# Linear attention and two feed-forward blocks on one core: the first group's attention over 128 tokens at once

## The chip, the cores and the metric

The kernel runs on one core of one Trainium2 chip. The metric is the device time of one execution in microseconds (us); lower is better. Engines are named as the profile names them: PE multiplies matrices (PEld is its weight load), DVE, ACT and POOL work on vectors, SP issues most of the transfers.

## The reference

Three blocks follow each other, over 2 batches of 768 tokens: attention with decay over 8 heads of 64, a feed-forward block of 2048, and a second block with a product of two projections. All data are float32.

```python
for b in range(nb):                      # blocks of 64 tokens
    intra = np.einsum('bhic,bhjc->bhij', qb, kb) * Dmask[None]
    intra = np.einsum('bhij,bhjd->bhid', intra, vb)
    inter = np.einsum('bhid,bhde->bhie', qb * lam_pow[None], kv_state)
    out[:, :, sl] = intra + inter
    kb_dec = kb * rev_pow[None]
    kv_state = lam_block[None, :, None, None] * kv_state + np.einsum('bhsd,bhse->bhde', kb_dec, vb)
...
h = x @ w_in; x = np.maximum(0.01 * h, h) @ w_out
...
out = ((x @ w1) * (x @ w2) @ w3) @ w_out2
```

`Dmask[i, j]` is `lam ** (i - j)` at and below the diagonal, `lam_pow[i]` is `lam ** (i + 1)`, `rev_pow[i]` is `lam ** (63 - i)`, and `lam_block` is `lam ** 64`. Attention is the same function for any block length; a longer block has fewer state updates and a larger mask.

## The kernel before

The 1536 tokens are 12 chunks of 128 and 3 groups of 512 (4 chunks a group, `CPG`). The 8 heads are 4 pairs (`NPAIR`); the two heads of a pair (`j` = 0, 1) lie on the two halves of the partitions.

The whole program is a list of operations, each with its engines, a cost on each, a rank and the buffers that it takes. `in_order` (L64) plays them against those costs and writes each operation to an engine when the plan says that it can start; the engine's instructions then stand in that order, and each engine works strictly in it. `LATENCY["q"]` and `MB` are the planner's figures for a transfer. They set the order alone.

**Attention** is `attention(n, rank, joined)` for chunk `n`. The chunk's queries, keys and values come in two transfers of 512 KB (L365): queries and keys transposed (parts 0, 1), then keys and values (parts 2, 3). Each half of 64 tokens is worked by itself. `front` makes 16 score products and up to 16 state products `kd` x values (64x64 each, on PE). `mask` (L388) multiplies the scores by the decay table `dm` on DVE, `q_decay` (L394) and `k_decay` (L403) scale queries and keys. `fade` and `update` (L453, L461) bring the state from one half to the next. `outs` makes 16 products of masked scores with values and up to 16 of scaled queries with the state. From the second chunk of a group on, the front of chunk `n` is written between the output products of chunk `n-1` (`scores`, L433), two products of the one and two of the other in turn; the last chunk's outputs stand alone (`outputs`, L523). `done` splits the result into a rounded part (ACT, L505) and the rest (DVE, L161) in the group's `xy`, which the first feed-forward block reads.

**For the first group** the flag `early` keeps `k_decay` on ACT and `q_decay` and `fade` on DVE.

**The feed-forward blocks** run on products of 128x128 by 128x512, each three times (rounded x rounded, rest x rounded, rounded x rest). `unit_h` (`full`, L534) reads all of a group's `xy`; `unit_y` (`products`, L541) sums into four accumulators. The weights come as 512 KB each (L230); `convert` rebuilds float32 from raw bits in two ACT passes (L235) and three DVE passes (L239, L245, L254), and `weight` splits it again (ACT L157, then DVE or POOL L161). The 4 weights of a block of `w_in` and the 4 of `w_out` are used for the three groups in turn. Chunks 4 to 11 are worked between these products.

The table code runs before all this: `load_lam` (L169) on SP, `pool_consts` on POOL, and `table` (L202), a running product on DVE, for `dm` and `lpow`.

Of the kernel before, what the change touches and what calls it, by code (L numbers as in the profile page):

```python
# [14 lines left out]
P = 128  # L15
# [5 lines left out]
T = 512  # L21
# [22 lines left out]
class Op:  # L44
# [6 lines left out]
    def __init__(self, cost, fn, rank, after=(), takes=(), uses=(), behind=(), port=False):  # L51
        self.cost, self.fn, self.rank, self.takes, self.behind, self.port = cost, fn, rank, takes, behind, port
        self.after = [o for o in after if o is not None]
        self.end = self.ready = None
        for b in (*takes, *uses):
            b.users.append(self)
# [3 lines left out]
LATENCY = {"q": 2000}  # L60
MB = 2800


def in_order(ops, depth, fixed):  # L64
# [33 lines left out]
    while n:  # L98
        for e in left:
            while free[e] <= now:  # L100
                shut = free["port"] > now
                shared = lambda c: e == "pool" or e == "dve" and c.port
                o = next((c for c in left[e][:400] if not (shut and shared(c)) and can(c)), None)
                if o is None:
                    break
                free[e] = o.end = now + o.cost[e]
                if shared(o):
                    free["port"] = o.end
                o.seen = o.end + LATENCY.get(e, 60)
# [13 lines left out]
def tile_kernel(ctx: ExitStack, tc, qkv, lamb, w_in, w_out, w1, w2, w3t, wo, out):  # L123
# [43 lines left out]
    def load_lam(e):  # L167
        T_["lam"] = const.tile([P, NPAIR], F32, name="lam_sb")
        nc.sync.dma_start(out=T_["lam"], in_=lamb)  # L169

    def pool_consts(e):

        T_["ident"] = const.tile([P, 2, D], F32, name="ident")
        T_["zero"] = const.tile([P, D], F32, name="zero")
# [7 lines left out]
            out=T_["ident"][:, 0, :], in0=T_["ident"][:, 0, :], in1=T_["ident"][:, 1, :], op=ALU.add  # L182
# [14 lines left out]
    def table(name, tag, first, data):  # L197

        def fn(e):
            T_[name] = const.tile([P, 512], F32, tag=tag, name=name)[:, : NPAIR * D].rearrange("q (p i) -> q p i", i=D)  # L200
            for p in range(NPAIR):
                nc.vector.tensor_tensor_scan(  # L202
                    T_[name][:, p, :], T_["lam"][:, p : p + 1].to_broadcast([P, D]), data(), first, ALU.mult, ALU.add
                )
        return fn
# [147 lines left out]

    def attention(n, rank, joined):
# [38 lines left out]
        def q_decay(e):  # L393
            engines[e].tensor_tensor(  # L394
                out=new(qd, [P, NPAIR, 2, D]), in0=t(0),
                in1=T_["lpow"].unsqueeze(2).to_broadcast([P, NPAIR, 2, D]), op=ALU.mult,
            )

        def k_decay(e):
# [12 lines left out]
        early = n < CPG  # L412
        k_op = op(
            {"act": 1250} if early else {"dve": 640, "pool": 1250, "act": 1250}, k_decay, rank,
            [ld[1], tables[0]], [kd], [inp], port=True,
        )
        q_op = op(
            {"dve": 640} if early else {"dve": 640, "pool": 1250}, q_decay, rank + 1, [ld[0], tables[1]], [qd], [inp],
            port=True,
# [46 lines left out]
        for c in range(2 if carry else 1):  # L466
# [3 lines left out]
            if old:  # L470
                fo = op({"dve": 420} if early else {"act": 1000, "dve": 420, "pool": 700}, fade(k, c), rank + 0.4, [st_op[k], tables[1]], port=True)
# [5 lines left out]
        px = Buf("acc" if early else "ps")  # L477
# [21 lines left out]
        def done(xo, behind=()):  # L499
            part = lambda v: xs[g].tile[:, v, :, c0 * CH : (c0 + 1) * CH]  # L500
            src = lambda: px.tile.rearrange("q p c i -> q p (c i)")
            r = xo.rank + 0.8

            def x_hi(e):
                nc.scalar.copy(part(0), src())  # L505

            o1 = op({"act": 580}, x_hi, r, [xo], [], [px, xs[g]])
            o2 = op({"dve": 660}, lo(lambda: part(1), lambda: part(0), src), r, [o1], [], [px, xs[g]], behind)
            x_ops[g] += [o1, o2]
            x_done[n] = xo  # L510
# [202 lines left out]
    def unit_o(g, f, rank):  # L713
# [32 lines left out]

    consts = op({"dve": 100}, dve_consts, 0)
    lam_op = op({"q": 400}, load_lam, 0.5)
    pc = op({"pool": 600}, pool_consts, 0)
    tables = [  # L750
        op({"dve": 900}, table("dm", "w34_6", 0.0, lambda: T_["ident"][:, 0, :]), 0, [lam_op, pc]),
        op({"dve": 900}, table("lpow", "w34_7", 1.0, lambda: T_["zero"]), 1, [lam_op, pc]),
    ]
    PLACE = {0: "yf0", 1: "yf1", 2: "yf2", 5: "yf1", 6: "yf2", 8: "yf1", 9: "yf2"}
    for n in range(CPG):
        attention(n, 10 * n, n > 0)
    outputs(CPG - 1, 10 * CPG)
# [4 lines left out]
    CHUNKS = {0: {4: 1, 5: 6}, 1: {6: 1, 7: 6}, 2: {8: 1}, 3: {9: 11}, 4: {10: 6}, 5: {11: 1}}  # L762
    for k in range(2):
# [34 lines left out]
def _lay_out(q, k, v, lam, moe_w_in, moe_w_out, moe2_w1, moe2_w2, moe2_w3, moe2_w_out):  # L798
# [15 lines left out]
    lamb = np.empty((P, NPAIR), lam.dtype)  # L814
    lamb[:D] = lam[0::2]
    lamb[D:] = lam[1::2]
# [29 lines left out]
```

## Time and profile before

| | |
|---|---|
| median of 3 runs | 559.92 us (558.36 to 560.97) |
| span of the profiled execution, first to last instruction | 556.9 us |
| that execution's own time | not recorded apart from the span; the three timed runs are 1.5 to 4.1 us longer than it |
| PE busy | 539.2 us, 97% of the span, 3680 products |
| DVE, ACT, POOL busy | 316.3, 301.4, 65.5 us |
| transfers | 54.07 MB, 97 GB/s in the mean |

Times in the rows below are us from the span's start. A row of the timeline gives start, length, engine, line, what is written and read, how many instructions it merges, and in brackets the idle time before it with what ended it. "issue" there means that the engine waited for nothing that the profile shows. Two engines' rows overlap freely; a busy engine that others wait for is what to look for.

### The profile page before, as it was taken

What the parts mean: (1) busy time and instruction counts of PE and PEld (TensorE: products, weight loads), DVE (VectorE), ACT (ScalarE), POOL (GpSimd) and SP (SyncE); (2) the same over time, 40 slices, a digit from 0 to 9 for tenths busy, and PEclk for the clock granted to TensorE, in tenths of its full rate; (3) what the DMA queues carried; (4) which work ended last, traced back from release to release, by engine and by line L of the source; (5) the groups of instructions that cost most, each with busy time, mean ns of one, the idle gap of its engine ahead of it and who ended that gap; (6) DMA issues with size and microseconds to landing.
All of it is one profiled execution on the core that took longest, in us unless ns stands there. A gap on an engine that the chain in (4) does not pass through costs nothing.

```text
span 556.9 us, 9041 instructions
## 1 busy us (share of the span) xinstructions
PE 539.2 (97%) x3680; PEld 447.1 (80%) x3680; DVE 316.3 (57%) x524; ACT 301.4 (54%) x540; POOL 65.5 (12%) x58
## 2 busy tenths in 40 slices
PE   5599999999999999999999999999999999999997
PEld 4488878888888888888888888888888888888885
DVE  4887798870348951699716778883233333343331
ACT  4787798892238742586724667763335333343331
POOL 0121040000000000020101201110003111120110
PEclk9899999999999999999999999999999999999999
DMA  8983845450004430146501324420002000020002
GB/s 287 385 286 107 288 171 191 150 185 5 0 4 142 157 114 0 39 151 207 171 1 38 114 79 149 151 77 0 1 0 77 1 1 0 2 75 1 0 0 77
DMA packets 15882, 54.07 MB, mean 97 GB/s; under 512 B 1888, under 2 KB 2144, under 8 KB 15840
## 3 DMA queue, kind: packets, MB, share of 16 engines
q1 hardware_dynamic: 15696, 53.36, 27.8%
q8 instruction: 29, 0.48, 0.3%
q10 hardware_dynamic: 144, 0.13, 0.1%
q14 instruction: 13, 0.11, 0.1%
HBM read 50.33 MB, written 3.15 MB: 96 GB/s over the span
## 4 chain that ended last, share of the span: by engine, by line
PE 89%; DMA 4%; DVE 3%; ACT 2%; issue 1%; SPq 1%; ACTq 0%
PE ps L534 45%; PE acc L541 34%; PE ps L672 8%; DMA raw<-in_w_in_dram 2%; DMA raw<-in_w_out_dram 1%; DMA yf<-in_qkv_dram 1%; PE ps L433 1%; PE ps L523 1%; DVE u L245 1%; ACT faded L449 1%; PE acc L433 1%; SPq L365 1%; DVE wa L161 0%; DVE f L254 0%; DVE rp L239 0%
## 5 line engine op out<-in xcount | busy, mean ns | idle before, releaser
L534 PE MATMUL ps<-xy,wp 128*128 128x512 f32 x756 | 179.1, 390 | 0.1
L534 PEld LDWEIGHTS ps<-xy,wp 128*128 128x128 f32 x756 | 141.8, 188 | 30.1 <-DVE a L388 0.5
L541 PE MATMUL acc<-act,wa 128*128 128x512 f32 x396 | 96.0, 390 | 0.0
L534 PE MATMUL ps<-xy,wa 128*128 128x512 f32 x396 | 95.5, 391 | 0.3 <-ACT wa L157 0.3
L534 PEld LDWEIGHTS ps<-xy,wa 128*128 128x128 f32 x396 | 74.0, 188 | 16.5 <-ACT wa L157 0.7
L541 PEld LDWEIGHTS acc<-act,wa 128*128 128x128 f32 x396 | 74.1, 188 | 15.5
L161 DVE TENSOR_TENSOR act<-ps,act 128x512 fp32r<-128x512 f32 x72 | 49.4, 686 | 59.0 <-ACT act L549 58.9
L541 PE MATMUL acc<-wp,act 128*128 128x512 f32 x276 | 66.6, 389 | 0.0
L157 ACT CAST wp<-wa 128x512 fp32r<-128x512 f32 x48 | 29.8, 622 | 63.8 <-PE ps L534 39.2
L235 ACT ACTIVATE rp<-raw,bp 128x512 f32<-128x512 uint16 x72 | 54.7, 764 | 15.2 <-DVE f L254 15.0
L541 PEld LDWEIGHTS acc<-wp,act 128*128 128x128 f32 x276 | 51.8, 188 | 10.7
L235 ACT ACTIVATE rn<-raw,bn 128x512 f32<-128x512 uint16 x72 | 54.6, 761 | 10.6 <-DMA raw<-in_w3t_dram 4.5
L570 ACT ACTIVATE ps<-ps 128x512 f32<-128x512 f32 x48 | 27.9, 580 | 57.8 <-PE ps L534 57.7
L239 DVE SCALAR_TENSOR_TENSOR rp<-rp,rn 128x512 uint32<-128x512 f32 x72 | 53.2, 740 | 4.5 <-ACT rp L235 3.8
L161 DVE TENSOR_TENSOR wp<-wa,wp 128x512 fp32r<-128x512 f32 x36 | 24.9, 691 | 49.7 <-ACT wp L157 49.7
L549 ACT CAST act<-ps 128x512 fp32r<-128x512 f32 x72 | 42.0, 583 | 5.6 <-DVE ps L708 2.9
L541 PE MATMUL acc<-act,wp 128*128 128x512 f32 x180 | 43.5, 391 | 0.0
L541 PEld LDWEIGHTS acc<-act,wp 128*128 128x128 f32 x180 | 33.6, 188 | 7.0
L254 DVE SCALAR_TENSOR_TENSOR f<-rp,u 128x512 uint32<-128x512 uint32 x56 | 38.6, 695 | 0.5
L245 DVE TENSOR_SCALAR u<-raw 128x512 uint32<-128x512 uint32 x72 | 34.0, 473 | 3.0 <-DMA raw<-in_w_in_dram 2.5
L708 DVE TENSOR_TENSOR ps<-ps,ta 128x512 f32<-128x512 f32 x24 | 16.8, 699 | 28.7 <-PE ps L534 28.7
L161 DVE TENSOR_TENSOR wp<-f,wp 128x512 fp32r<-128x512 f32 x24 | 16.6, 690 | 26.6 <-ACT wp L157 26.6
(92 smaller groups left out, 524.5 us busy)
## 6 DMA issues: line engine op xcount, KB each, us to landing
raw<-in_w_in_dram SPq DMA_DIRECT2D x16, 512.0 KB, 4.4
raw<-in_w_out_dram SPq DMA_DIRECT2D x16, 512.0 KB, 4.1
raw<-in_w3t_dram SPq DMA_DIRECT2D x16, 512.0 KB, 4.2
raw<-in_w_dram SPq DMA_DIRECT2D x16, 512.0 KB, 3.3
yf<-in_qkv_dram SPq DMA_DIRECT2D x14, 512.0 KB, 6.1
inp<-in_qkv_dram SPq DMA_DIRECT2D x10, 512.0 KB, 6.7
raw<-in_wo_dram SPq DMA_DIRECT2D x8, 512.0 KB, 4.1
out_dram<-f SPq DMA_DIRECT2D x11, 256.0 KB, 2.0
```

What stands on the lines that cost most here:

```text
L157: return lambda e: nc.scalar.copy(dst(), src())
L161: engines[e].tensor_tensor(out=dst(), in0=src(), in1=hi_().bitcast(F32), op=ALU.subtract)
L235: nc.scalar.activation(out=new(buf, [P, 512]), in_=top, func=AF.Relu, scale=8.0, bias=T_[bias])
L239: nc.vector.scalar_tensor_tensor(out=rp.tile.bitcast(U32), in0=rp.tile, scalar=32768.0, in1=rn.tile, op0=ALU.min, op1=ALU.add)
L245: nc.vector.tensor_scalar(out=new(u, [P, 512], U32), in0=mid, scalar1=2.0**-13, scalar2=2.0**19 - 1, op0=ALU.mult, op1=ALU.min)
L254: nc.vector.scalar_tensor_tensor(out=get().bitcast(U32), in0=rp.tile.bitcast(U32), scalar=16, in1=u.tile, op0=ALU.logical_shift_left, op1= ...
L534: nc.tensor.matmul(o, w(a)[:, cc * P : (cc + 1) * P], x(b, cc), start=k == 0, stop=k == 3 * NCC - 1)
L541: nc.tensor.matmul(o, st(a), mv(b), start=first and k == 0, stop=last and k == 2)
L549: nc.scalar.copy(buf.tile[:, 0, :], ps.tile)
L570: nc.scalar.activation(out=ps.tile, in_=ps.tile, func=AF.Prelu, alpha=0.01)
L672: nc.tensor.matmul(ps.tile, w(a)[:, k * P : (k + 1) * P], wo_part[j](b), start=j == 0 and n == 0, stop=j == NF2 - 1 and n == 2,)
L708: lambda e: nc.vector.tensor_tensor(out=pb.tile, in0=pb.tile, in1=ta.tile, op=ALU.mult),
```

## The change

Chunks 0 to 3 get a function of their own, `first_attention`, with all 128 tokens of a chunk as one block. Scores are 8 products of 128x128 for a chunk, the state 8 of 64x64 (over 128 tokens), the outputs 8 of 64x128 from the masked scores and 8 of 64x128 from the state. There is one fade and one state update for a chunk. Masks are two DVE operations of 512 a partition, with two new tables `wide0` and `wide1` of 128 columns a pair; `lpow` gets 128 columns too, and `dm` is built later. `k_decay` takes 8 ACT operations of 64 instead of 4 of 128. `q_decay` and `fade` may go to POOL. No front is written between another chunk's outputs any more. `lamb` is loaded from ACT's queue, with 12 columns instead of 4. The host lays out parts 2 and 3 of the first four chunks with 128 tokens on the partitions. The weight `("in", 0)` gets rank 25, and the planner's two transfer figures change.

```diff
-LATENCY = {"q": 2000}
-MB = 2800
+LATENCY = {"q": 3600}
+MB = 2900
...
-        nc.sync.dma_start(out=T_["lam"], in_=lamb)
+        nc.scalar.dma_start(out=T_["lam"], in_=lamb)
...
+    def wide_table(j):
+        def fn(e):
+            T_["wide", j] = const.tile([P, NPAIR, CH], F32, name=f"wide{j}")
+            for p in range(NPAIR):
+                k = NPAIR + 2 * p + j
+                nc.vector.tensor_tensor_scan(
+                    T_["wide", j][:, p, :], T_["lam"][:, k : k + 1].to_broadcast([P, CH]),
+                    T_["ident"].rearrange("q x y -> q (x y)"), 0.0, ALU.mult, ALU.add,
+                )
...
+    def first_attention(n, rank):
...
+        def scores(e):
+            for j in range(2):
+                new(sc[j], [P, NPAIR, CH])
+            for p in range(NPAIR):
+                for j in range(2):
+                    h = half[j]
+                    mm(sc[j].tile[:, p, :], rows(1)[h, p, :], rows(0)[h, p, :], start=True)
+        fr = op({"pe": 1300}, scores, rank, [ld[0]], [*sc], [inp])
...
+        masked = [op({"dve": 660}, mask(j), rank, [fr, wide[j]], [a[j]], [sc[j]]) for j in range(2)]
...
+            q_op = op({"dve": 640, "pool": 1250}, q_decay, rank + 1, [ld[0], tables[1]], [qd], [inp], port=True)
...
+        k_op = op({"act": 2100, "dve": 800}, k_decay, rank + 1, [ld[1], *wide], [kd], [inp], port=True)
...
+                for j in range(2):
+                    mm(st.tile[half[j], 0, p, :], kd.tile[:, p, j, :], heads(3)[:, p, j, :], start=True)
+        st_mm = op({"pe": 700}, sums, rank + 1, [k_op], [st], [inp, kd])
...
+            fo = op({"act": 1000, "dve": 420, "pool": 700}, fade, rank + 0.4, [st_op[2 * n], tables[1]], port=True)
...
+        st_op[2 * n + 2] = op({"dve": 420}, update, rank + 0.5, [st_mm, fo, x_done.get(n - 2)], [], [st])
...
+            for kind in ("v", "state") if inter else ("v",):
+                for p in range(NPAIR):
+                    for j in range(2):
+                        o = px.tile[half[1 - j], p, :]
+                        if kind == "v":
+                            mm(o, heads(3)[:, p, j, :], a[j].tile[:, p, :], start=p == 0)
+                        else:
+                            mm(o, state(2 * n)[half[j], p, :], qd.tile[half[j], p, :], start=False)
...
     for n in range(CPG):
-        attention(n, 10 * n, n > 0)
-    outputs(CPG - 1, 10 * CPG)
+        first_attention(n, 10 * n)
...
+    weight("in", 0, 0, 25)
```

Where the order moves, in the places that the prediction speaks of:

PE, from the last chunk of the first group to the second wide product block, before (`acc<-a` and `acc<-qd` are chunk 3's outputs, `ps<-inp` and `ps<-inp,kd` chunk 4's front, `ps<-xy,wa` is `unit_h`):

```order
L523 MATMUL acc<-a,inp 64x64 x2
L523 MATMUL acc<-qd,state_115 64x64 x2
L433 MATMUL ps<-inp 64x64 x16
L433 MATMUL ps<-inp,kd 64x64 x16
L534 MATMUL ps<-xy,wa 128x512 x24
```

The same place now (L393 is the first group's attention: `acc<-a` and `acc<-ta` are chunk 3's outputs from its two masks; its eight state products, `acc<-inp,kd`, stand two rows above this piece):

```order
L393 MATMUL acc<-ta,inp 64x128
L393 MATMUL acc<-a,inp 64x128
L393 MATMUL acc<-ta,inp 64x128
L393 MATMUL acc<-a,inp 64x128
L393 MATMUL acc<-ta,inp 64x128
L393 MATMUL acc<-a,inp 64x128
L393 MATMUL acc<-ta,inp 64x128
L393 MATMUL acc<-qd,state_117 64x128 x8
L676 MATMUL ps<-xy,wa 128x512 x12
L585 MATMUL ps<-inp 64x64 x16
L585 MATMUL ps<-inp,kd 64x64 x16
L676 MATMUL ps<-xy,wa 128x512 x12
```

Chunk 4's front now follows the first `unit_h` instead of preceding it, and 120 small products stand ahead of that block (8+8+8 for the first chunk and 8 more for each other), where 248 of chunks 0 to 3 and 32 of chunk 4 stood.

ACT, from chunk 3's `k_decay` to the last rounding of the first group's `xy`, before:

```order
L403 ACTIVATE kd_349<-inp_258,dm_125 128x2x64 x4
L505 CAST xy_199<-acc_279 128x4x128
L157 CAST wa_362<-f_355 128x512
L235 ACTIVATE rp_366<-raw_273,bp_101 128x512
L235 ACTIVATE rn_370<-raw_273,bn_103 128x512
L235 ACTIVATE rp_443<-raw_345,bp_101 128x512
L235 ACTIVATE rn_446<-raw_345,bn_103 128x512
L403 ACTIVATE kd_451<-inp_357,dm_125 128x2x64 x4
L505 CAST xy_199<-acc_378 128x4x128
L403 ACTIVATE kd_468<-yf1_373,dm_125 128x2x64 x4
L235 ACTIVATE rp_512<-raw_460,bp_101 128x512
L235 ACTIVATE rn_515<-raw_460,bn_103 128x512
```

and now:

```order
L427 ACTIVATE kd_305<-inp_217,wide0_126 128x64 x4
L427 ACTIVATE kd_305<-inp_217,wide1_132 128x64 x4
L453 ACTIVATE faded1_122<-state1_117,lpow_149 128x64 x4
L158 CAST wa_364<-f_343 128x512
L502 CAST xy_208<-acc_324 128x4x128
L251 ACTIVATE rp_387<-raw_253,bp_103 128x512
L251 ACTIVATE rn_391<-raw_253,bn_105 128x512
L502 CAST xy_208<-acc_369 128x4x128
```

Before, the `k_decay` of chunks 4 and 5 and five more weight passes stood ahead of the last rounding; now a fade, one weight split and two weight passes do.

## Rows read from the trace of the kernel before

**Rows 1.** The page: busy times, PE in 40 slices, the queue of instructions.

```profile
PE 539.2 (97%) x3680; PEld 447.1 (80%) x3680; DVE 316.3 (57%) x524; ACT 301.4 (54%) x540; POOL 65.5 (12%) x58
...
PE   5599999999999999999999999999999999999997
...
q8 instruction: 29, 0.48, 0.3%
```

**Rows 2.** Waits of PE from 0 to 31 us: total, times, longest.

```profile
PE ps L433 <- DMA yf<-in_qkv_dram: 5.3, 2, 4.9
PE acc L433 <- issue: 4.4, 2, 3.6
PE ps L433 <- ACT kd L403: 1.3, 1, 1.3
PE acc L523 <- issue: 1.2, 1, 1.2
```

**Rows 3.** Timeline of PE, single rows between 4 and 42 us.

```profile
4.94 1.97 PE L433 MATMUL ps<-yf 64*64 64x64 f32 x32 [4.94 <-DMA yf<-in_qkv_dram]
...
22.57 0.37 PE L433 MATMUL acc<-qd,state 64*64 64x64 f32 x2 [3.61 <-issue]
...
28.62 0.98 PE L433 MATMUL ps<-inp 64*64 64x64 f32 x27
29.43 1.10 PE L433 MATMUL ps<-inp,kd 64*64 64x64 f32 x32
30.46 5.75 PE L534 MATMUL ps<-xy,wa 128*128 128x512 f32 x24
...
41.49 3.01 PE L534 MATMUL ps<-xy,wa 128*128 128x512 f32 x12 [0.31 <-ACT wa L157]
```

**Rows 4.** Windows: length, busy (instructions) of PE, PEld, DVE, ACT, POOL, clock, DMA share, GB/s.

```profile
0.00:16.38 16.38, 8.12 (x222) 7.55 (x222) 8.60 (x24) 7.24 (x17) 1.10 (x8) 1.00 0.85 305
16.38:22.56 6.18, 2.35 (x127) 2.08 (x127) 4.91 (x11) 4.85 (x10) 0.00 (x0) 0.99 1.02 402
22.56:28.03 5.47, 4.24 (x127) 4.11 (x128) 4.25 (x9) 4.10 (x11) 1.71 (x2) 0.70 0.92 348
```

**Rows 5.** Windows after the wide products began, same columns.

```profile
30.46:100.00 69.54, 69.17 (x1130) 56.75 (x1127) 57.96 (x102) 56.49 (x121) 11.89 (x10) 1.00 0.60 207
100.00:310.00 210.00, 210.00 (x928) 173.96 (x927) 126.30 (x208) 115.70 (x194) 12.14 (x9) 1.00 0.27 88
```

**Rows 6.** Timeline of ACT, 17 to 35 us.

```profile
17.58 1.28 ACT L403 ACTIVATE kd<-inp,dm 128x128 f32<-128x128 f32 x4 [1.59 <-DMA inp<-in_qkv_dram]
18.77 0.56 ACT L505 CAST xy<-acc 128x512 fp32r<-128x512 f32 x1
19.23 0.62 ACT L157 CAST wa<-f 128x512 fp32r<-128x512 f32 x1
19.75 0.76 ACT L235 ACTIVATE rp<-raw,bp 128x512 f32<-128x512 uint16 x1
20.41 0.75 ACT L235 ACTIVATE rn<-raw,bn 128x512 f32<-128x512 uint16 x1
...
33.62 1.05 ACT L449 ACTIVATE faded<-state,lpow 128x64 f32<-128x64 f32 x4
34.58 0.57 ACT L570 ACTIVATE ps<-ps 128x512 f32<-128x512 f32 x1
```

**Rows 7.** Timeline of DVE and POOL, single rows.

```profile
5.17 0.84 DVE L202 TENSOR_TENSOR_SCAN dm<-lam_sb,ident 128x64 f32<-128x64 f32 x4 [4.21 <-DMA lam_sb<-in_lamb_dram]
...
29.49 0.69 DVE L161 TENSOR_TENSOR xy<-acc,xy 128x512 fp32r<-128x512 f32 x1 [0.34 <-ACT xy L505]
...
71.48 1.76 POOL L394 TENSOR_TENSOR qd<-inp,lpow 128x512 f32<-128x512 f32 x1 [12.37 <-issue]
```

**Rows 8.** The chain that ended last: wide blocks of 12, start, length.

```profile
87.30 2.95 PE acc L541 x12
...
100.65 2.72 PE acc L541 x12
```

More of the change, by code (lines that the diff above doesn't have):

```diff
@@ L44, with __init__ @@
 class Op:
-    def __init__(self, cost, fn, rank, after=(), takes=(), uses=(), behind=(), port=False):
+    def __init__(self, cost, fn, rank, after=(), takes=(), uses=(), behind=(), port=False, lag=None):
         self.cost, self.fn, self.rank, self.takes, self.behind, self.port = cost, fn, rank, takes, behind, port
@@ L108, in in_order @@
                     free["port"] = o.end
-                o.seen = o.end + LATENCY.get(e, 60)
+                o.seen = o.end + (o.lag or LATENCY.get(e, 60))
                 n -= 1
@@ L181, in pool_consts @@
         nc.gpsimd.tensor_tensor(
-            out=T_["ident"][:, 0, :], in0=T_["ident"][:, 0, :], in1=T_["ident"][:, 1, :], op=ALU.add
+            out=T_["ident64"], in0=T_["ident"][:, 0, :], in1=T_["ident"][:, 1, :], op=ALU.add
         )
@@ L195, in dve_consts, with table @@
         nc.scalar.activation(out=T_["warm"], in_=T_["bp"], func=AF.Relu)
-    def table(name, tag, first, data):
+    def table(name, tag, first, data, wide):
         def fn(e):
-            T_[name] = const.tile([P, 512], F32, tag=tag, name=name)[:, : NPAIR * D].rearrange("q (p i) -> q p i", i=D)
+            T_[name] = const.tile([P, 512], F32, tag=tag, name=name)[:, : NPAIR * wide].rearrange(
+                "q (p i) -> q p i", i=wide
+            )
             for p in range(NPAIR):
                 nc.vector.tensor_tensor_scan(
-                    T_[name][:, p, :], T_["lam"][:, p : p + 1].to_broadcast([P, D]), data(), first, ALU.mult, ALU.add
+                    T_[name][:, p, :], T_["lam"][:, p : p + 1].to_broadcast([P, wide]), data(), first, ALU.mult, ALU.add
+                )
+        return fn
+    def wide_table(j):
[6 more added lines that the diff above has]
+                    T_["ident"].rearrange("q x y -> q (x y)"), 0.0, ALU.mult, ALU.add,
                 )
@@ L354, in attention, with x_split, x_hi @@
+    def x_split(n, xo, px, src, behind=()):
+        g, c0 = divmod(n, CPG)
+        part = lambda v: xs[g].tile[:, v, :, c0 * CH : (c0 + 1) * CH]
+        r = xo.rank + 0.8
+        def x_hi(e):
+            nc.scalar.copy(part(0), src())
+        o1 = op({"act": 580}, x_hi, r, [xo], [], [px, xs[g]])
+        o2 = op({"dve": 660}, lo(lambda: part(1), lambda: part(0), src), r, [o1], [], [px, xs[g]], behind)
+        x_ops[g] += [o1, o2]
+        x_done[n] = xo
     def attention(n, rank, joined):
@@ L395, in q_decay @@
                 out=new(qd, [P, NPAIR, 2, D]), in0=t(0),
[L396 removed]
+                in1=T_["lpow"][:, :, :D].unsqueeze(2).to_broadcast([P, NPAIR, 2, D]), op=ALU.mult,
             )
@@ L470, in attention @@
             if old:
-                fo = op({"dve": 420} if early else {"act": 1000, "dve": 420, "pool": 700}, fade(k, c), rank + 0.4, [st_op[k], tables[1]], port=True)
+                fo = op({"act": 1000, "dve": 420, "pool": 700}, fade(k, c), rank + 0.4, [st_op[k], tables[1]], port=True)
             st_op[k + 1] = op({"dve": 420}, update(k + 1, c, old), rank + 0.5, [fr, fo, x_done.get(n - 2)], [], [st])
@@ L499, in done @@
         def done(xo, behind=()):
[L500 to L510, printed above, removed]
+            x_split(n, xo, px, lambda: px.tile.rearrange("q p c i -> q p (c i)"), behind)
         pend[n] = {
@@ L813, in _lay_out @@
     qkv = np.stack([transposed(q), transposed(k), natural(k), natural(v)], axis=2)
-    lamb = np.empty((P, NPAIR), lam.dtype)
-    lamb[:D] = lam[0::2]
-    lamb[D:] = lam[1::2]
+    for part, a in ((2, k), (3, v)):
+        whole = a.reshape(B, NPAIR, 2, NCHB, CH, D).transpose(0, 3, 4, 1, 2, 5).reshape(nch, P, 512)
+        qkv[:CPG, :, part] = whole[:CPG]
+    lamb = np.empty((P, NPAIR + H), lam.dtype)
+    lamb[:D, :NPAIR] = lam[0::2]
+    lamb[D:, :NPAIR] = lam[1::2]
+    lamb[:, NPAIR:] = lam
     w_in = moe_w_in.reshape(NPAIR, 2, D, F1)[:, ::-1].reshape(DM, F1)
```

99 lines of the change are left out of this document (88 added, 11 removed).

## The prediction

> **What bounds the kernel now.** Read the page first. PE is busy for 97% of the span, and its slices are full from the third on; only the first two, 28 us, have room [rows 1]. Then the windows: from 30.46 us, where the first wide product starts [rows 3], to 100 us PE is busy 69.17 of 69.54 us, and from 100 to 310 us all of the time [rows 5]. So the time is the moment at which the wide products start plus PE's own work behind it, 556.9 - 30.46 = 526.4 us with the last copies. The change can gain ahead of 30.46 us, and lose by giving PE more work or a wait behind it.
>
> Ahead of it the list of waits names what PE lacks [rows 2]: 5.3 us for queries, keys and values (4.9 of them the first load), 1.3 us for scaled keys, and 5.6 us (4.4 + 1.2) of "issue", in which neither data nor a semaphore is late. The windows show where these pauses sit: cut at their ends, they hold 222+222 = 444, then 127+127 = 254, then 127+128 = 255 instructions of PE and PEld [rows 4]. The page has 7360 of them over the kernel and 29 packets of 0.48 MB in the queue of instructions, 254 instructions and 16.5 KB for each [rows 1]. So PE stops where a new packet of its code is due, and does so while it runs through small products quickly and the transfers run at 402 GB/s. [...]
>
> **The new chain to the first wide product.** Loads keep their order and their bytes, and they run at the limit of the transfers (402 GB/s [rows 4]: 524 KB in 1.30 us), so I leave them where they are; without `lam`, SP is free 0.4 us sooner at most, which I count as nothing. Chunk 3's last half lands at 17.58 us: there ACT's wait ends and `kd` begins [rows 6]. From then on ACT's own list, in the order shown above, leads to the end:
> - `kd`, 8 operations of 64, and a fade, 4 more. Four such operations take 34.58 - 33.62 = 0.96 us to the next instruction [rows 6]: 3 x 0.96 = 2.88 us, to 20.46.
> - a weight split, 19.75 - 19.23 = 0.52 us, and the rounding of chunk 2's outputs, 19.23 - 18.77 = 0.46 us: to 21.44.
> - two weight passes of 20.41 - 19.75 = 0.66 us: to 22.76.
> - the rounding of chunk 3's outputs, 0.56 us, to 23.32, and on DVE the rest, 0.69 us [rows 7]: 24.0.
>
> PE must have chunk 3's outputs ready by 22.76. The trace has no 128-column form of these products. The nearest row is a front at the full clock, 32 instructions in 1.10 us [rows 3], which are 8 pairs of 64 columns, 0.14 us a pair; with twice the columns I take 0.28. The low end is 0.14 (length costs nothing), the high end about 0.5 (the two heads do not overlap, or all runs as slowly as the first 32, 1.97 us [rows 3]: 0.25 a pair, doubled 0.49). At 0.28, chunk 3's state products take 4 x 0.14 = 0.55 us from 19.50 (`kd` ready), its outputs 8 x 0.28 = 2.2 us: 22.3, within 0.5 us of late.
>
> On that stretch lies one more packet of code. 120 small products make 480 instructions ahead of the first wide one, where 280 made 1120, so of three pauses one is left, near the 445th instruction. That is in chunk 3's outputs. It can cost 0 (the packet is there) to 3.61 us. I take 0.5 us behind what ACT's list covers: the pause at the same count was the short one, 4.4 - 3.6 = 0.8 us [rows 2], and about 0.5 is covered, but the products now come to it faster. The wide products then start at 24.5 us, 5.96 us earlier.
>
> [...]
>
> **What is covered.** Tables: four running products of 64 columns take 0.84 us [rows 7]; the two wide tables and `lpow` have twice the columns, 0.84 to 1.68 us each, so all are done by 5.2 + 3 x 1.68 = 10.2 us at the latest, and the loads of the last two chunks hide it; the end hangs on chunk 3, at 16.3 us and later. `q_decay` on POOL takes up to 1.76 us [rows 7] where DVE took less; chunk 3's queries land one transfer before 17.58, at 16.3, and are wanted near 21.2. If POOL's two fades come first, 1 us of that cover goes and nothing shows. DVE's list up to the last rest (two masks, an update, two rests, three weight passes, none over 0.7 us) runs beside ACT's 5.7 us.
>
> **What moves behind the start.** Chunk 4's front, 30.46 - 28.62 = 1.84 us [rows 3], stood ahead of the wide products and now stands among them: all of it is added. It also makes two more changes between small and wide products: a block of 12 beside such a change takes 2.95 us, one without 2.72 [rows 8], so 0.23 us. The other chunks keep their products.
>
> **The sum.** -5.96 + 1.84 + 0.23 = -3.9 us: 556.9 becomes 553.0. The timed runs lie 1.5 to 4.1 us above the span, 3.0 for the median, which I carry over: 559.9 - 3.9 = **556.0 us**. No change, for a measurement of this kernel, is within 0.5%, 2.8 us.
>
> **The rivals.**
>
> *The small products stay slow, and the kernel is slower.* At the lower clock, or with the two heads of a pair one after the other, a 128-column pair takes the high end, 0.49 us. Scores, outputs and state outputs are then 1.97 us each for a chunk, the state products 0.98. Four chunks take 25.6 us, less a state output for the first; the second chunk lands six transfers of 1.30 us before 17.58, at 9.8 us, and 23.6 us are left then. PE ends at 33.4, the wide products start at 34.6, 4.2 us late, and with the 2.07 us behind them the time is 566.2. It decides from the third chunk on: each chunk at that speed costs 3.4 us more, so two of them eat the gain. For it: the first 32 instructions took 1.97 us against 1.10 later [rows 3], though the granted clock reads 1.00 there [rows 4]. Against it: PE ran at speed in the window up to the long pause, 127 products in 2.35 us [rows 4], with waits for loads and weights before that it will have less of, and it slowed only behind 3.61 us of nothing. [...]
>
> *The pause of code stays at full length.* With 3.6 us at the 445th instruction, reached near 21 us, outputs end at 25.9 instead of 22.3, and the wide products start at 27.1: -3.4 + 2.07 = -1.3 us, 558.6. For it: the longest pause of before came at the same rate of transfers [rows 4].
>
> *The conversions become the bound.* The wide products start 6 us earlier, but the weights are still converted at ACT's pace. Per two weights ACT has four passes, two splits and two operations on the result, 4 x 0.66 + 2 x 0.52 + 2 x 0.57 = 4.8 us, and per chunk `kd`, a rounding and two fades, 1.19 + 0.46 + 1.92 = 3.6 us [rows 6]: 8.4 us against PE's 2 x 2.72 + 1.84 = 7.3. Four such steps lose 4.4 us, of which the two `kd` that the new order gives to POOL take 2.4 away: 2.0 to 4.4 us lost, 558.0 to 560.4. For it: the one wait of the wide products is for a weight, 0.31 us [rows 3], with DVE busy 57.96 and ACT 56.49 of 69.54 us [rows 5].
>
> **How the numbers follow.** The forecast gets 0.60, the slow products 0.11, the pause 0.13, the conversions 0.16. The forecast's own range: 0 for the code pause and 0.5 us less on ACT give 555.0, transfers 0.4 us sooner and first wide products that begin on the rounded part alone, 0.69 us before the rest [rows 7], give 553.9, and the scatter of the runs of before, about 1 us, 553; upward, pause and cover together 1.5 us, 557.5. To hold 8 in 10 the range reaches over the pause and the conversions and leaves most of the slow products out: 553.0 to 560.4. Faster by over 0.5% (below 557.1) is 0.54 of the forecast and 0.04 of the pause and the conversions, where they come in part: 0.58. Within 0.5% is the rest of these, 0.06 + 0.25 = 0.31. Slower by over 0.5% is the first rival, 0.11.
>
> **What the profile of the changed kernel should show.** The first wide product near 24.5 us; ACT's last rounding of chunk 3 near 23; one "issue" pause in the first group, under 1 us, near the 445th instruction; a pair of scores at 0.28 us; chunk 4's front of 1.84 us between the first two wide blocks; no wait over 0.5 us of a wide product for a weight. It is wrong if the wide products start after 28 us, or if waits for weights between 25 and 60 us add up to more than 2 us.

## The result, and the profile after

| | before | after |
|---|---|---|
| median | 560.12 us (558.36 to 560.97, 4 runs) | 553.69 us (553.47 to 555.85, 4 runs) |
| ratio, 95% interval | | 0.9895 (0.9867 to 0.9923) |
| span of the profiled execution | 556.9 us | 551.8 us (its own time: 553.47 us) |
| PE's product instructions | 3680 | 3424 |

The kernel is 6.4 us faster, 556.0 was forecast. The two profiled spans differ by 5.1 us only: the profiled execution after took 1.7 us more than its span, as later runs did (1.7 to 2.0), so the one of before, 556.9 + 1.7 = 558.6 us, was 1.5 us faster than its median.

The page of the changed kernel, engines, PE's slices, its clock and the instruction queue, to be held against [rows 1] (an attention product takes two instructions of PE, x16 for eight scores below, a wide one takes one):

```profile
PE 540.8 (98%) x3424; PEld 447.5 (81%) x3424; DVE 313.4 (57%) x522; ACT 305.7 (55%) x564; POOL 67.9 (12%) x61
...
PE   5899999999999999999999999999999999999997
...
PEclk9999999999999999999999999999999999999999
...
q8 instruction: 27, 0.44, 0.3%
```

The second slice fills, and PE is busy 1.6 us longer than before although it has 256 instructions, 128 products, less. The clock row reads 9 throughout; the upper level, 1.00, holds from 12.65 us on (below). Its waits over the whole execution, against [rows 2] (us in total, times, longest):

```profile
PE ps L393 <- DMA yf<-in_qkv_dram: 5.9, 2, 5.1
PE ps L676 <- DVE xy L162: 0.7, 1, 0.7
PE ps L676 <- ACT xy L502: 0.7, 1, 0.7
```

No pause named "issue" is left, and no wait for a weight. PE's timeline, against [rows 3] (`first_attention` is L393, `full` L676, `products` L683, later fronts L585):

```profile
5.10 2.08 PE L393 MATMUL ps<-yf 64*128 64x128 f32 x16 [5.10 <-DMA yf<-in_qkv_dram]
7.95 2.08 PE L393 MATMUL ps<-yf 64*128 64x128 f32 x16 [0.77 <-DMA yf<-in_qkv_dram]
9.96 1.12 PE L393 MATMUL acc<-yf,kd 128*64 128x64 f32 x16
...
12.57 0.68 PE L393 MATMUL acc<-yf,kd 128*64 128x64 f32 x16
13.18 1.16 PE L393 MATMUL ps<-yf 64*128 64x128 f32 x16
...
21.56 1.09 PE L393 MATMUL acc<-qd,state 64*64 64x128 f32 x16
23.34 0.73 PE L676 MATMUL ps<-xy,wa 128*128 128x512 f32 x2 [0.69 <-ACT xy L502]
24.80 2.55 PE L676 MATMUL ps<-xy,wa 128*128 128x512 f32 x10 [0.73 <-DVE xy L162]
27.28 1.15 PE L585 MATMUL ps<-inp 64*64 64x64 f32 x32
28.26 1.10 PE L585 MATMUL ps<-inp,kd 64*64 64x64 f32 x32
29.29 3.02 PE L676 MATMUL ps<-xy,wa 128*128 128x512 f32 x12
...
547.27 0.84 PE L683 MATMUL acc<-xy,act 128*128 128x512 f32 x3
```

PE has no idle time from 7.95 to 22.65 us. What was gained ahead of the first wide product is waiting: the kernel before waited 13.3 us there, 12.2 in [rows 2] and 1.1 in the line

```profile
PE acc L433 <- DVE a L388: 1.1, 2, 0.9
```

and worked 17.2 us, 1.84 of them chunk 4's front; the changed kernel waits 6.6 us (5.9 + 0.7) and works 16.8. So 6.7 us of waits are gone, 5.6 of which were pauses named "issue", and chunk 4's front has moved away; the first group's own products take PE 16.8 us now and took 15.3.

The clock needs care here. The trace's records of the granted clock begin only at 12.65 us (12.19 in the kernel before); ahead of the first record, a 1.00 in a row stands for no record. A product of the outputs takes 0.42 us up to there and 0.27 behind it, and the scores 2.08 and 1.16. Experiment 6 has the same scores where the clock is recorded, at its lower level of 0.50, and there they take 2.08 us again (timeline; then a window of PE alone with length, busy, clock, DMA share, GB/s):

```profile
26.89 2.08 PE L394 MATMUL ps<-inp 64*128 64x128 f32 x16
```

```profile
26.89:28.89 2.00, 2.00 (x17) 0.50 0.00 0
```

So by these lengths PE, idle until its first data came at 5.10 us, began at the lower level. In all 14 profiles of this document the products change their length at the first record of the clock, between 6.1 and 16.0 us; this moves the start of the wide products from profile to profile.

The account of the span: the first wide product comes at 23.34 instead of 30.46 (-7.1); behind it stand chunk 4's front, 29.29 - 27.28 = 2.0 us, and 1.0 us that two products lose ahead of the other ten (24.80 - 23.34 less 2 x 0.227, a twelfth of the 2.72 us of a block in [rows 8]); 0.7 us of stalls at 41 and 82 us are gone, of which [rows 3] show one. PE's last product ends at 548.11 us, before at 552.86 (-4.75), and the tail behind it is 0.35 us shorter: -5.1.

ACT's timeline, which my chain went along, and DVE's and POOL's just ahead of the wide products:

```profile
16.43 0.58 ACT L502 CAST xy<-acc 128x512 fp32r<-128x512 f32 x1 [0.42 <-PE acc L393]
16.91 2.02 ACT L427 ACTIVATE kd<-inp,wide 128x64 f32<-128x64 f32 x8
...
22.70 0.58 ACT L502 CAST xy<-acc 128x512 fp32r<-128x512 f32 x1 [0.48 <-PE acc L393]
```

```profile
22.29 1.26 DVE L261 TENSOR_SCALAR u<-raw 128x512 uint32<-128x512 uint32 x1
23.47 0.68 DVE L255 SCALAR_TENSOR_TENSOR rp<-rp,rn 128x512 uint32<-128x512 f32 x1
24.07 0.68 DVE L162 TENSOR_TENSOR xy<-acc,xy 128x512 fp32r<-128x512 f32 x1
```

```profile
22.21 1.05 POOL L562 TENSOR_TENSOR kd<-inp,dm 128x512 f32<-128x512 f32 x1
```

`kd` of chunk 3 starts at 16.91 us without a wait for its data; both of ACT's waits here are for PE. The rest of chunk 3 (24.07) stands on DVE behind two passes for a weight, of which the first took 1.26 us while POOL scaled keys, and 0.42 in the median of its 72.

### The profile page after: what moved, and what is told of

Its sections match the earlier page's. It is cut to its first block, busy times and chain, and to the rows that moved or that the text cites. A ratio compares the mean times of both kernels' runs of the same rounds, so it can differ in the third digit from the quotient of the medians.

```text
span 551.8 us, 8567 instructions
## 1 busy us (share of the span) xinstructions
PE 540.8 (98%) x3424; PEld 447.5 (81%) x3424; DVE 313.4 (57%) x522; ACT 305.7 (55%) x564; POOL 67.9 (12%) x61
## 4 chain that ended last, share of the span: by engine, by line
PE 97%; DMA 1%; DVE 1%; SPq 0%; issue 0%; ACT 0%; DVEq 0%
PE ps L676 48%; PE acc L683 36%; PE ps L814 8%; PE ps L585 3%; PE acc L393 2%; DMA yf<-in_qkv_dram 1%; PE ps L393 1%; PE ps L665 1%; DVE xy L162 0%; DVE u L261 0%; SPq L383 0%; DVE rp L255 0%; DVE wa L162 0%; DVE f L876 0%; DVE state L465 0%
## 5 line engine op out<-in xcount | busy, mean ns | idle before, releaser
L676 PE MATMUL ps<-xy,wp 128*128 128x512 f32 x756 | 178.9, 389 | 0.0
L676 PEld LDWEIGHTS ps<-xy,wp 128*128 128x128 f32 x756 | 141.8, 188 | 29.7
L676 PE MATMUL ps<-xy,wa 128*128 128x512 f32 x396 | 95.8, 391 | 1.4 <-DVE xy L162 0.7
L683 PE MATMUL acc<-act,wa 128*128 128x512 f32 x396 | 95.8, 390 | 0.0
L676 PEld LDWEIGHTS ps<-xy,wa 128*128 128x128 f32 x396 | 73.8, 188 | 18.0 <-DVE xy L162 1.6
L683 PEld LDWEIGHTS acc<-act,wa 128*128 128x128 f32 x396 | 74.0, 188 | 15.5
L683 PE MATMUL acc<-wp,act 128*128 128x512 f32 x276 | 66.6, 389 | 0.0
L683 PEld LDWEIGHTS acc<-wp,act 128*128 128x128 f32 x276 | 51.8, 188 | 10.8
L255 DVE SCALAR_TENSOR_TENSOR rp<-rp,rn 128x512 uint32<-128x512 f32 x72 | 50.5, 702 | 8.8 <-ACT rn L251 6.7
L683 PE MATMUL acc<-act,wp 128*128 128x512 f32 x180 | 43.4, 390 | 0.0
L270 DVE SCALAR_TENSOR_TENSOR f<-rp,u 128x512 uint32<-128x512 uint32 x56 | 40.9, 737 | 0.3
L683 PEld LDWEIGHTS acc<-act,wp 128*128 128x128 f32 x180 | 33.7, 188 | 7.0
L850 DVE TENSOR_TENSOR ps<-ps,ta 128x512 f32<-128x512 f32 x24 | 16.8, 700 | 29.9 <-PE ps L676 29.9
L261 DVE TENSOR_SCALAR u<-raw 128x512 uint32<-128x512 uint32 x72 | 31.6, 443 | 3.1 <-DMA raw<-in_w_out_dram 2.3
L775 DVE TENSOR_TENSOR yf<-acc,yf 128x512 f32<-128x512 f32 x36 | 23.8, 688 | 13.4 <-PE acc L683 13.4
```

Of the source, the lines that this page charges most:

```text
L255: nc.vector.scalar_tensor_tensor(out=rp.tile.bitcast(U32), in0=rp.tile, scalar=32768.0, in1=rn.tile, op0=ALU.min, op1=ALU.add)
L261: nc.vector.tensor_scalar(out=new(u, [P, 512], U32), in0=mid, scalar1=2.0**-13, scalar2=2.0**19 - 1, op0=ALU.mult, op1=ALU.min)
L270: nc.vector.scalar_tensor_tensor(out=get().bitcast(U32), in0=rp.tile.bitcast(U32), scalar=16, in1=u.tile, op0=ALU.logical_shift_left, op1= ...
L676: nc.tensor.matmul(o, w(a)[:, cc * P : (cc + 1) * P], x(b, cc), start=k == 0, stop=k == 3 * NCC - 1)
L683: nc.tensor.matmul(o, st(a), mv(b), start=first and k == 0, stop=last and k == 2)
L775: nc.vector.tensor_tensor(out=yf[g][:, c, :], in0=acc.tile, in1=yf[g][:, c, :], op=ALU.add)
```

## Experiments

The times of before beside them are 559.16 (15 runs, first four), 560.09 (13, next four), 559.97 (7, next three) and 559.18 us (7, the last).

**1. Products cut in two.** Scores and outputs of 64 columns instead of 128 (the edit of the scores; that of the outputs is alike):

```diff
-mm(sc[j].tile[:, p, :], rows(1)[h, p, :], rows(0)[h, p, :], start=True)
+for c in range(2):
+    s = slice(c * D, c * D + D)
+    mm(sc[j].tile[:, p, s], rows(1)[h, p, :], rows(0)[h, p, s], start=True)
...
```

> The changed kernel with every score and output product of the first group written as two products of 64 columns instead of one of 128: the same columns, 208 small products instead of 120 ahead of the first wide one, 832 instructions of PE and PEld instead of 480. Theory (the gain comes from fewer instructions, which spare the pauses where a new packet of code is due): the issue pauses come back, 2 of them before the wide products, 1 to 4 us in all; the wide products start at 24.5 to 27.5 us instead of 23.3; time 555 to 558 us. Rival (the pauses had another cause, and the gain is order and loads): no issue pause over 0.3 us, start at 23.3 to 24, time within 1 us of the changed kernel's 553.7.

558.17 us (10 runs, 0.998 of before, 0.9966 to 0.9994): nearly the whole gain is gone. But not by pauses; there is none named "issue". PE's timeline, and the window between its 445th and 701st instruction (columns as in [rows 4]):

```profile
4.85 7.15 PE L393 MATMUL ps<-yf 64*128 64x64 f32 x64 [4.85 <-DMA yf<-in_qkv_dram]
...
19.99 2.05 PE L393 MATMUL ps<-inp 64*128 64x64 f32 x32
...
28.46 0.73 PE L680 MATMUL ps<-xy,wa 128*128 128x512 f32 x2 [0.68 <-ACT xy L506]
```

```profile
19.78:25.36 5.58, 5.51 (x135) 5.15 (x132) 3.53 (x6) 4.61 (x16) 1.27 (x1) 1.00 0.90 319
```

A chunk's scores take 2.05 us in 16 products, and in 8 (13.18 us, above) 1.16: they go by the number, not by the columns. The outputs do not: those from the masked scores of a chunk take 1.08 us in 16 products (22.49 to 23.57) and 0.98 in 8 (17.92 to 18.90 in the changed kernel). The wide products start 28.46 - 23.34 = 5.1 us later by PE's own time, without any pause. About 4 us of that are the products, an estimate from 0.9 us of scores and 0.2 of outputs in each chunk; in this profile the clock also rose later, at 15.95 us instead of 12.65. The time was as the theory had it up to 0.2 us, the reason was not; both theories miss here. Nor does this run measure the kernel before, where a chunk's half has 16 state products of 64x64 in 1.10 us [rows 3].

**2. The table back on SP's queue**, planned between the two transfers of chunk 0 as before.

```diff
-nc.scalar.dma_start(out=T_["lam"], in_=lamb)
+nc.sync.dma_start(out=T_["lam"], in_=lamb)
...
```

> The changed kernel with the table of decay factors loaded by SP again, between the two transfers of chunk 0, as before the change. My prediction counted this at 0.4 us at most, hidden. Since PE is busy without a gap from the landing of chunk 1's first half (7.95 us) to the wide products, a rival says that what the loads lose PE loses: chunk 1's first half near 8.4 to 8.95 us, wide products 0.4 to 1.0 us later, time 0.4 to 1.0 us up. By the prediction's count: less than 0.3 us.

555.97 us (6 runs, 0.9939, 0.9918 to 0.9961), 2.3 us above the changed kernel. All of the change without the table's queue is thus worth 559.16 - 555.97 = 3.2 us, and the queue, which I put at nothing, the other 2.3, to within the few tenths by which medians differ. What all queues had moved in the first 8 us, in the kernel before, here, and in the changed kernel:

```profile
DMA packets 616, 1.75 MB, mean 219 GB/s; under 512 B 189, under 2 KB 189, under 8 KB 616
```

```profile
DMA packets 577, 1.60 MB, mean 200 GB/s; under 512 B 187, under 2 KB 187, under 8 KB 577
```

```profile
DMA packets 676, 1.98 MB, mean 248 GB/s; under 512 B 194, under 2 KB 194, under 8 KB 676
```

The table is 128 packets of 48 bytes, 6 KB. With it in SP's queue 0.38 MB less had moved, which at the 402 GB/s of [rows 4] is 0.95 us; the same edit in the kernel before (experiment 5) moved 324 GB/s in the mean of the first 15.58 us, instead of 300. Why, no run tells: SP's next issues come 0.4 us later, which is less than that, and the table's own packets took 11 ns each in the changed kernel. PE's second scores then start at 9.38 instead of 7.95 us, the first wide product at 25.33 instead of 23.34:

```profile
9.38 2.08 PE L393 MATMUL ps<-yf 64*128 64x128 f32 x16 [2.49 <-DMA yf<-in_qkv_dram]
...
25.33 0.73 PE L676 MATMUL ps<-xy,wa 128*128 128x512 f32 x2 [0.69 <-ACT xy L502]
```

Of these 2.0 us, 1.4 are the later data; the other 0.6 are the clock, which rose at 15.27 us in this profile, 5.9 us behind the start of the second scores instead of 4.7, with PE working all the while. Whether it does so in every execution is not known.

**3. The planner's figures and the early weight taken back.**

```diff
-LATENCY = {"q": 3600}
-MB = 2900
+LATENCY = {"q": 2000}
+MB = 2800
-    weight("in", 0, 0, 25)
```

> The changed kernel with the planner's two transfer figures of before (2000 and 2800) and the first weight not asked for at rank 25: the order of before's planner, with the new products. Theory (the products' number makes the gain): wide products start within 0.7 us of 23.3 us, time 553 to 554.7 us. Rival (the early weight and the order make it): a wait of the first wide products for a weight of over 1 us, time above 556 us.

553.05 us (4 runs, 551.72 to 553.95). First wide product at 23.30 us, a wait of 0.8 us for a weight behind. The theory holds: these parts of the change give nothing that can be measured.

**4. Products of zeros at the start.**

```diff
+if n == 0:
+    for _ in range(12):
+        mm(sc[0].tile.rearrange("q p i -> q (p i)")[:, :P], T_["zero"], T_["zero"], start=True)
...
```

> The changed kernel with 12 products of zeros, 128x128 by 128 columns, ahead of the first scores, while PE has nothing to do; their result is overwritten by the scores. The first 7 us of products are half as fast as later ones (scores of a chunk 2.08 us at 5.10 us, 1.16 us at 13.18 us). Theory (PE's own slow start is what bounds the stretch to the wide products, since PE has no idle time from 7.95 to 22.65 us): scores of chunk 0 and 1 in 1.1 to 1.2 us, wide products 1.0 to 2.3 us earlier, time 551.4 to 552.7 us. Rival (ACT's list bounds it, as my prediction had it): the scores are faster, ACT's roundings end when they did, wide products within 0.5 us of 23.3, time within 0.5 us of 553.7. Third: the speed does not depend on work ahead of it, and nothing changes.

553.07 us (4 runs, 552.70 to 554.57). PE, then ACT:

```profile
6.47 1.16 PE L394 MATMUL ps<-yf 64*128 64x128 f32 x16
7.86 1.16 PE L394 MATMUL ps<-yf 64*128 64x128 f32 x16 [0.23 <-DMA yf<-in_qkv_dram]
...
22.79 0.73 PE L680 MATMUL ps<-xy,wa 128*128 128x512 f32 x2 [1.36 <-ACT xy L506]
24.41 2.56 PE L680 MATMUL ps<-xy,wa 128*128 128x512 f32 x10 [0.89 <-DVE xy L163]
```

```profile
16.97 2.02 ACT L431 ACTIVATE kd<-inp,wide 128x64 f32<-128x64 f32 x8 [1.19 <-DMA inp<-in_qkv_dram]
...
22.15 0.58 ACT L506 CAST xy<-acc 128x512 fp32r<-128x512 f32 x1
```

The scores run at full speed from the first chunk on (the clock's records begin at 6.51 us here), and PE ends 1.2 us earlier, but the wide products only 0.55: now ACT waits for chunk 3's landing and its list leads, as I had forecast for the changed kernel. That is nearer to the rival; PE's slow start, which is the lower clock, and ACT's list lie 0.55 us apart.

**5. Only the table's queue changed, in the kernel before** (the edit of 2, the other way).

> The kernel before with one thing of the change: the table of decay factors is loaded from ACT's queue instead of SP's. In the changed kernel the same step was worth 2.3 us (554.0 against 551.8 us of span). Theory (in the kernel before, PE's pauses of code set the pace from 16 us on, so that earlier data only lengthens them): loads about 1 us earlier, issue pauses together 0.5 to 1.5 us longer than 5.6, time 558.5 to 560 us. Rival (the loads set the pace there too): wide products 1.5 to 2.3 us earlier than 30.46, time 557 to 558 us.

559.10 us (10 runs, 0.9983, 0.9963 to 1.0004). First wide product at 30.31 us, "issue" 4.4 + 1.4 us. The time and the start are as the theory had them, but the pauses are 0.2 us longer, not 0.5 to 1.5. The two blocks of PE's code behind the first pause took 6.56 and 5.76 us, where [rows 4] have 6.18 and 5.47, the first of them in part at the lower clock:

```profile
15.58:22.14 6.56, 3.48 (x127) 3.34 (x127) 4.45 (x9) 4.93 (x11) 0.00 (x0) 0.76 1.02 387
```

So most of the 0.8 us by which PE reached the first of them earlier was lost in these two blocks, partly in pauses and partly in slower work. Of the queue's 2.3 us at most 2.1 can be had without the new products, by the interval, and nothing clear of the noise was.

**6. A burst of small products.**

```diff
+if n == 3:
+    for i in range(128):
+        h = half[i % 2]
+        mm(sc[i % 2].tile[h, 0, :8], T_["zero"][h, :D], T_["zero"][h, :8], start=True)
```

> The changed kernel with 128 products of zeros, 64x64 by 8 columns, ahead of the scores of chunk 3, which overwrite them: 512 more instructions of PE and PEld, run through quickly. In the kernel before, each pause ended 2.4 to 2.5 us after a packet of code had begun to move (14.03, 20.14 and 25.54 against 16.39, 22.57 and 28.05), and packets came 5.4 to 6.1 us apart. Theory (256 instructions in less than 5.4 to 6.2 us make a pause, whatever they compute): the burst itself takes 2.5 to 4.5 us, and one or two issue pauses of 2 to 6 us in all come in or behind it; wide products at 27 to 32 us. Rival (no pause, since nothing but the length of the work counts): no issue pause over 0.5 us, wide products 2.5 to 4.5 us later than 23.3.

567.71 us (4 runs, 1.0138, 1.0114 to 1.0163). No pause named "issue" came, but as a test of pauses it says nothing, since the burst was far slower than I took it to be:

```profile
16.84 10.12 PE L394 MATMUL ps<-zero 64*64 64x8 f32 x244
```

```profile
20.00:21.00 1.00, 1.00 (x42) 1.00 1.02 410
21.00:22.00 1.00, 1.00 (x28) 0.53 1.01 401
22.00:23.00 1.00, 1.00 (x24) 0.50 1.05 410
```

(windows of PE alone: length, busy, clock, DMA share, GB/s.) Up to 21 us one of PE's instructions starts every 28.5 ns (110 from 16.84 to 20 us); two for a product make 57 ns for a product of 8 columns, all written to the same places. The kernel before ran 127 instructions in 2.35 us [rows 4], 37 ns for a product of 64. And at 21 us, while PE had run nothing but these since 16.84, the clock fell to the lower level, 0.50.

**7 and 8. Chunk 3's rounding and rest first**, and the same with the zeros of 4: operations of two weights and of chunk 4 may be planned only behind them.

```diff
-o2 = op({"act": 680}, relu(rn, "bn"), rank, [o0, consts], [rn], [raw])
+x3 = x_ops[0][-2:] if len(loads) in (2, 3) else []
+o2 = op({"act": 680}, relu(rn, "bn"), rank, [o0, consts], [rn], [raw], behind=x3[:1])
...
```

> The changed kernel with chunk 3's rounding and rest written ahead of what ACT and DVE do for the next two weights and for chunk 4 (a rounding pass for each weight, two passes on DVE, q_decay and k_decay of chunk 4). In the changed kernel the first wide product stood at 23.34 us, and ten of twelve waited until 24.80 for the rest on DVE, which came behind two passes of a weight (1.26 and 0.68 us). Theory (PE's outputs end at 22.65, then rounding and rest one after the other): rounding as before, rest 0.6 to 1.0 us earlier, the ten products from 23.9 to 24.2 us, time 552.7 to 553.2 us. Rival (the weights are then late): a wait of over 0.5 us for a weight behind chunk 4's front, time 553.5 us or more.

> The orders of the run above together with the 12 products of zeros at the start. PE's outputs of chunk 3 ended at 21.4 us in the run with zeros, but ACT's rounding came at 22.15 and DVE's rest at 24.4, behind the weights' passes. Theory (each hides the other): rounding at 21.5, first wide product at 22.0, the others from 22.6 to 22.9 us, time 551.0 to 551.8 us. Rival (the landing of chunk 3 or the next weights bound it): less than 0.6 us below the run with zeros alone, 552.5 us or more.

554.24 us (4 runs, 0.9901, 0.9878 to 0.9925) and 554.40 (4, 0.9898, 0.9870 to 0.9925): no gain. The first twelve wide products run in one go, from 22.50 in the first (where the clock rose at 11.09 us, which is not the edit's doing), but later PE waits for a weight that moved back:

```profile
22.50 3.29 PE L680 MATMUL ps<-xy,wa 128*128 128x512 f32 x12 [0.68 <-ACT xy L503]
...
47.13 2.80 PE L680 MATMUL ps<-xy,wp 128*128 128x512 f32 x11 [1.15 <-DVE wp L162]
```

Both rivals are right: what DVE does for the next weights has little to spare.

**9. Transfers held, in the kernel before.** One small transfer on SP's queue that waits for chunk 3's rounding, and all later loads behind it:

```diff
+nc.sync.dma_start(out=T_["hold"], in_=xs[0].tile[:, 0, 0, -1:].bitcast(F32))
...
```

> The kernel before with every transfer behind chunk 3's, apart from the first weight's, held on SP's queue until chunk 3's outputs are rounded (a transfer of 512 bytes reads them first). Its time is of no interest, the next weights come late; the stretch up to the first wide product is. Over the runs so far, PE never took less than 5.5 us from the 445th to the 701st instruction while the transfers ran at 400 GB/s (6.18 us in the kernel before, 6.56 with the table on ACT's queue, 5.56 with split products, 5.67 in the burst). Theory (the packets of code share the way with the data and wait there): no data moves from about 15 us on, the issue pauses add up to less than 1.5 us instead of 5.6, and the 256 instructions take less than 4 us. Rival (code comes at its own rate of one packet in 5.4 to 6.1 us): issue pauses of 4 us or more in all, the 256 instructions in 5.4 us or more.

570.06 us (1 run), the weights being late. Windows cut at the 445th, 701st and 957th instruction, against [rows 4]:

```profile
0.00:16.87 16.87, 8.47 (x222) 8.01 (x222) 9.18 (x26) 7.34 (x17) 1.11 (x8) 0.99 0.79 279
16.87:20.43 3.56, 3.53 (x129) 3.40 (x129) 2.42 (x5) 1.68 (x6) 0.00 (x0) 0.55 0.04 14
20.43:24.48 4.05, 2.83 (x129) 2.69 (x130) 3.95 (x10) 1.17 (x3) 0.00 (x0) 1.00 0.02 4
```

Of its waits, one line is left for such pauses:

```profile
PE acc L433 <- issue: 1.3, 1, 1.3
```

The first pause, while chunk 3 still loads, is there; behind it hardly anything moves, and the pauses of 3.61 and 1.2 us are gone, though PE takes a block of its code in 3.56 us where it had taken 6.18. So they are waits of code behind data: the theory holds. Of the four values named in the expectation, those of the split products and of the burst were PE's own work without a pause (5.51 us busy, at 319 GB/s, in the first) and show no such wait. The trace's packets of code show where the wait lies. With the transfers held, a packet began to move 1.2 us after PE had entered a block (18.08 against 16.87, 21.64 against 20.43); in the kernel before it was 3.8 and 3.0 us (20.14 against 16.38, 25.54 against 22.56). From there to the end of a pause it was 2.3 to 2.5 us in both. So the next block would have been there some 3.6 us after the last, an estimate from 1.2 and 2.4. PE, at the lower clock for most of the block (0.55 in the mean), took as long for its work, 3.53 us; whether it would pause at the upper clock with the transfers held, no run shows.

**10 to 12. A version that keeps the weights' order.** Zeros as in 4, and of the second weight three operations moved, nothing else (the place where the order is written):

```diff
+held = [x for x in plan if x[0] in second]
+rest = [x for x in plan if x[0] not in second]
+for x in reversed(held):
+    at = next(i for i, y in enumerate(rest) if y[0] is x_ops[0][-2 if x[1] == "act" else -1]) + 1
+    rest.insert(at, x)
```

`second` holds the weight's second ACT pass and its first two DVE passes. 11 is the changed kernel again, 12 the order without the zeros.

> The changed kernel with 12 products of zeros at the start and three operations of the second weight (one pass on ACT, two on DVE) written behind chunk 3's rounding and rest; everything else in the order of the run with zeros alone, 551.4 us of span. Theory (the two waits of 1.36 and 0.89 us before the wide products there are ACT's and DVE's order alone): first wide product at 22.0 to 22.4 us, all twelve in one go, no wait for a weight behind, time 1.0 to 1.8 us below the changed kernel beside it. Rival (the weights are converted at a pace that leaves nothing to an earlier start): a wait of about 1 us for a weight between 30 and 60 us, time within 0.6 us of the changed kernel.

> The changed kernel itself once more, beside the others of this call: 553.2 to 554.2 us.

> The changed kernel with the order of the fastest run so far (three operations of the second weight behind chunk 3's rounding and rest), but without the products of zeros: it parts the 1.75 us between the two. Theory (the order takes away the one wait between the first two and the other ten wide products, 0.73 us in one profile of the changed kernel and none in the other): all twelve products in one go, time 553.0 to 553.8 us, so most of the 1.75 us is the zeros'. Rival (the order makes it): 552.4 us or less.

10: 552.07 us (4 runs, 551.58 to 552.64; 0.9848 of before, 0.9811 to 0.9885); 11: 553.82 (4 runs, 553.44 to 555.22); 12: 552.70 (4 runs, 551.73 to 554.64; 0.9862, 0.9821 to 0.9903). Version 10 beats both kernels, by 1.75 us the changed one beside it; whether zeros or order make it is not told apart: 12 lies between what its theory and its rival had. In 10 the first wide product came at 22.90, not at 22.0 to 22.4, in one go with the rest and with no wait behind. Run 11 shows that the changed kernel itself varies:

```profile
22.35 3.29 PE L676 MATMUL ps<-xy,wa 128*128 128x512 f32 x12 [0.69 <-ACT xy L502]
...
55.94 0.68 PE L585 MATMUL ps<-yf,kd 64*64 64x64 f32 x15 [1.71 <-issue]
```

There the start came 1.0 us earlier, without a wait for DVE, and 1.71 us were lost to a pause of code in a later chunk's front, at 316 GB/s; the span was 552.0 us all the same. Most of the earlier start is the clock: it rose at 10.90 us instead of 12.65, and from the second scores to the first wide product PE took 14.7 us instead of 15.4. Run 12's profile has a pause of 1.7 us too. That such pauses and the moment of the clock's rise make the scatter of the changed kernel's times (553.4 to 555.9 us over its eight runs) is likely, but not shown.

## Why the prediction was right, and where it was not

The direction, the range and the main account (earlier start of the wide products as PE's pauses go, less chunk 4's front) were right. How near the time came is luck in part: two terms were off the same way by more than the 2.3 us between forecast and median, and what the chain left out offset some of it.

- **"I leave them where they are ... which I count as nothing"**, of the loads without the table on SP: the mis-sized term. It measured 2.3 us in time (experiment 2). I had the 0.4 us of SP's issue and not the 0.38 MB that the loads are then behind. That this equals the miss is chance, as the next two points show.
- **3.0 us around the span** was too much: it is 1.7, and the profile of before was 1.5 us faster than its median. Without that the forecast would have been 1.3 us nearer. On spans, -3.9 stood against -5.1; of these 1.2 us some 0.2 lie in the start and the front, 0.7 in the stalls that went at 41 and 82 us and 0.35 in the tail, and I had forecast neither stalls nor tail.
- **The start at 24.5 us**, all twelve products fed, was nearly right: 23.34 for two and 24.80 for the other ten are as good as 24.3. But with the table back on SP, which is what I had counted with, they came at 25.33 and 26.36, as good as 25.9. So the chain was about 1.4 us short, and the table's gain made up for it.
- **ACT's list from chunk 3's landing** did not lead; PE did, from 7.95 us on, and up to 12.65 at the lower clock. The list itself was sized well: 17.58 to 23.32 is 5.74 us by my sum, and 16.97 to 22.73 is 5.76 in experiment 4, where it leads. In the changed kernel it is the next bound, 0.55 us below.
- **A pair of scores at 0.28 us**: 0.29 (1.16 us for four). But the first two chunks ran at 0.52 (2.08 for four), the high end that I gave to the first rival, and for its first reason, the lower clock; the 1.00 that I read in [rows 4] is no record there. The rival was right about them and wrong from the third chunk on, where I said it would be decided.
- **0.5 us of pause near the 445th instruction**: none there, as PE now takes 7.27 us over about a block; the window:

```profile
13.95:21.22 7.27, 7.27 (x134) 6.34 (x131) 5.96 (x12) 6.84 (x25) 1.90 (x2) 1.00 1.03 412
```

  The reason behind it, that the gain is pauses avoided by a smaller count, fits: 5.6 of the 6.7 us of waits that went were such pauses, and experiment 9 shows them to be waits of code. Experiment 1 does not show that the count alone removes them, as its products, twice as many, were too slow to make a pause.
- **Chunk 4's front**: 2.0 us for 1.84 + 0.23. Right.
- **The conversions as bound**: not in the changed kernel, which has no wait for a weight. They are what ended experiments 7 and 8.
- The wait of ten products for chunk 3's rest, 0.7 us, was not in the forecast: I had DVE's list as covered, and missed that a weight's two passes would be planned ahead of the rest, one of them three times as long beside POOL's product.

## What to carry to other kernels

Where a start is bound by data and small products, count four things apart: PE's work (by the form of its products; here a chunk's scores went by their number, 2.05 us in 16 products and 1.16 in 8, and its outputs rather by their columns, 1.08 and 0.98), blocks of code (in the kernel before PE paused ahead of its 445th, 701st and 957th instruction, PEld's counted in, each time until 2.4 to 2.5 us after a packet of code had begun to move; these came 5.4 to 6.1 us apart beside transfers at 397 to 414 GB/s), the clock (here at its lower level up to 12.65 us, by scores of 2.08 us and then 1.16), and what else stands in the queue of the first loads. A table of 6 KB cost 2.3 us in the queue of the first large loads here; try it in another engine's. And check what an execution's own time adds to its span before carrying a difference over; one profile is one draw.

## What was not expected of the hardware

- With a 6 KB table in 48-byte packets on the queue of the loads, 0.38 MB less had moved after 8 us (experiment 2); why is open.
- Packets of code wait behind data: a block of PE's code took 6.18 us at 402 GB/s and 5.47 at 348 [rows 4], pauses included, and 3.56 without a pause with the transfers held (14 GB/s). The wait lies ahead of the packet's first byte: 3.0 to 3.8 us against 1.2.
- The first products run at the lower clock while the rows of the clock read 1.00, as no record exists ahead of the first: 2.08 us for scores at 5.10 and 7.95, 1.16 at 13.18, and 2.08 again where 0.50 is recorded (experiment 6). With 12 products of zeros ahead they took 1.16 from the start.
- A product of 8 columns took 57 ns, no less than one of 64 (37 ns, from [rows 4]), and the clock fell to its lower level, 0.50, at 21 us though PE had been busy with such products throughout, from 16.84 us on.
